# Soft-MoE experts stage: 256-column halves of the last weights, transposes moved, TensorE's order written out, filler products

## Chip, cores and metric

The kernel runs on one core of one Trainium2 chip, as one launch. The metric is the device time of one execution in microseconds; the median of three runs of the kernel before is 974.0 us (lowest 972.54, highest 979.01). Less is better.

## The reference

Three layers run one after the other; B is 8, H is 8, S is 576, N is 4608 tokens of 512 numbers.

```python
attn = softmax(mask(q @ k.T / 8)) @ v            # block-causal, blocks of 64
x = attn.transpose(0, 2, 1, 3).reshape(N, 512)
logits = x @ phi                                 # phi 512 x 32: 8 experts, 4 slots each
d = softmax(logits, axis=0)                      # over the tokens
slot_input = (d.T @ x).reshape(8, 4, 512)
for e in range(8):                               # w1[e] 512 x 1024, w2[e] 1024 x 512
    slot_out[e] = relu(slot_input[e] @ w1[e]) @ w2[e]
x = softmax(logits, axis=1) @ slot_out.reshape(32, 512)
h = relu(x @ w_in)                               # w_in 512 x 2048
out = (h * h) @ w_out                            # w_out 2048 x 512
```

The MoE weights are 32 MiB of float32 and `w_out` comes as 8 MiB of 64-bit floats (the device decodes them to float32), so the middle of the kernel moves much and computes little: 32 slots only.

## The kernel before, in words

**Stages.** `attention` (L195) runs over 32 pairs of heads (8 batches of 4). With each batch it updates a running maximum, a running sum `tot` and the running slot input `acc` (L69). `experts` (L1017) turns `acc` into slot outputs. `ffn` (L1196) is the long last stage: 96 steps of 18 products of 128x128 by 128x512 (L1306 to L1308), on TensorE alone nearly all of the time.

**The last batch's chain.** After the last pair the list `last` (L836 to L838) has one long chain of small steps: the logits of the last pair, `maxes` (VectorE), `running` (a transpose L726, then VectorE L728 to L731), `weights` (a product L737, VectorE, then ScalarE's exponentials L745 and L746), `total` (L786), `gather` (L815, L821), `invert` (L801, then VectorE L803 to L805), and the update of `acc` in four pieces (L828). `tokens` (L756) transposes the tokens of the batch beside it. Line 1013 issues what is left of the batch's work and then `last`, outside of the `manual_schedule` of L1009.

**Experts.** There are 32 weight chunks of 1 MiB (`wlist`, L147): 8 of `w1` for experts 0 to 3, 8 of `w1` for experts 4 to 7, 8 of `w2` for experts 0 to 3, and 8 of `w2` for experts 4 to 7. Each lies in a slot named by a letter (`slots`, L82). 19 chunks (RING) have a slot of their own; chunk 19 and on take a slot over when the products that read it are done. `after(r)` (L1079) issues the load of chunk r+19 behind the products of chunk r, on SyncE's queue, in the order of the chunks; behind chunk 31 come the first four tiles of `w_out` (`fetch_wo`, L1140), each MiB with 4 KB rows.

Chunks 0 to 23 are read from memory in rows of 2 KB. The last eight (L129 to L137) are quarters of columns: chunk c has column block `dt = c // 2` of 128 columns and one half of the 1024 rows of `w2`, for four experts; each of its four DMAs (256 KB, rows of 512 bytes) has 128 rows of all four experts. So each output block of 128 columns is complete after two chunks, is copied (L1130), transposed (`finish`, L1060) and folded with `w_in` into `psw` (`fold`, L1070: 4 products of 512 columns) while the next chunks come in. Behind the last chunk stand one copy, one transpose, one small copy (L1065) and one fold.

For each of four half layers the hidden values are copied with the Relu (L1096) and transposed at once (L1099). The softmax over experts for all tokens (`combine_a`, `combine_c` on VectorE, `combine_b` on TensorE: six transposes L1193 and a copy L1194 for each of six token groups) is spread over the chunks with `put`: `combine_b(g)` stands behind chunk 16+2g (CSTART 14, CSTEP 2).

**What sets TensorE's order.** Inside `manual_schedule` for TensorE (L1009) its instructions stay in the order of the program. Outside of it, in `experts` and `ffn` too, the compiler's scheduler orders them by its own estimate. The other engines' instructions are ordered by that scheduler in either case.

**Head of ffn.** L1208 issues the decoding of the first `w_out` tile (`decode_wo(0)`: one ScalarE and four VectorE steps, L154 to L180), then `psw` is split into `wf` (L1214 to L1219, ScalarE, VectorE and GpSimd), spread over the partitions (L1243), and the first hidden tile follows (L1252, L1262 to L1270).

A float32 product stands in the trace as two MATMUL records, one of a 16-bit type as one.

Of the kernel before, what the change touches and what calls it, by code (L numbers as in the profile page):

```python
# [23 lines left out]
def tile_attn_soft_moe_ffn(  # L24
# [27 lines left out]
    CSTART = 14  # L52
    CSTEP = 2
# [43 lines left out]
    nxt = [0]  # L97
    wots = {}
# [10 lines left out]
    def wchunk(i):  # L109
        kind, g, c = wlist[i]  # L110
        nm = slots[i]
        if nm in fixed:
            runs = [ar[:, 512 * q0:512 * (q0 + nq)] for ar, q0, nq in fixed[nm]]
        else:
            runs = [wpools[nm].tile([128, 2048], F32, tag="w", name="wch")]
        wt[i] = []
        fs = []
        for t in runs:
            nq = t.shape[1] // 512
            e0 = 4 * g + len(wt[i])  # L120
            es = slice(e0, e0 + nq)
            qs = [t[:, 512 * x:512 * x + 512] for x in range(nq)]
            wt[i] += qs
            if kind == 0:
                fh, dt = divmod(c, KD)
                src = w1[es, 128 * dt:128 * dt + 128, 512 * fh:512 * fh + 512].rearrange("e p f -> p e f")
            elif g == 0:
                src = w2[es, 128 * c:128 * c + 128, :].rearrange("e p f -> p e f")
            else:  # L129
                dt, kh = divmod(c, 2)  # L130
                for x in range(nq):
                    r0 = 512 * kh + 128 * (e0 - 4 * g + x)
                    src = w2[4 * g:4 * g + 4, r0:r0 + 128, 128 * dt:128 * dt + 128]
                    fs.append(lambda o=qs[x], src=src: nc.sync.dma_start(
                        out=o.rearrange("p (e f) -> p e f", e=4), in_=src.rearrange("e p f -> p e f")
                    ))
                continue  # L137
            if nm in "01" and i < RING:
                for x in range(nq):
                    fs.append(lambda o=qs[x], src=src[:, x]: nc.sync.dma_start(out=o, in_=src))  # L140
            else:
                fs.append(lambda t=t, src=src, nq=nq: nc.sync.dma_start(
                    out=t.rearrange("p (e f) -> p e f", e=nq), in_=src
                ))
        return fs
# [49 lines left out]
    def attention():  # L195
# [442 lines left out]
        def batch(b):  # L638
# [192 lines left out]

            if b == B - 1:
# [3 lines left out]
                    [lambda: logits_pair(3), maxes, running, groups] + [lambda u=u: tokens(u, 3) for u in range(5)]  # L836
                    + [recycle, weights, total] + [lambda u=u: gather(u) for u in range(4)] + [invert, lambda: gather(4)]
# [174 lines left out]
        nxt[0] += 1  # L1012
        for f in dq + work + half[1:] + last:
            f()
        st.close()

    def experts():  # L1017
# [19 lines left out]
        nc.vector.tensor_copy(si[:, :, 0:NSL], ps[:, 0:128].rearrange("p (a s) -> p a s", a=KD))  # L1037
        psw = ps_w.tile([128, 512], F32, tag="dx", name="psw")
# [4 lines left out]
        todo = {CSTART: [setup_sel]}  # L1043
# [4 lines left out]
        for g in range(NTILE // NG):  # L1048
            put(CA + g, lambda g=g: combine_a(g))
            put(CSTART + CSTEP * g, lambda g=g: combine_c(g))  # L1050
            put(
                CSTART + 2 + CSTEP * g,
                lambda g=g: combine_b(ps_e.tile([128, 1024], F32, tag="c", name="ps_c", bufs=1), g),
            )

# [28 lines left out]

        for g in range(2):
            for fh in range(2):
                for dt in range(KD):
                    for e4 in range(4):
# [4 lines left out]
                        )  # L1093
                    after(8 * g + KD * fh + dt)
                hs = ep.tile([128, 512], F32, tag="hs", name="hs")
                nc.scalar.activation(out=hs, in_=hp_[fh], func=AF.Relu)  # L1096
                pt = ps_e.tile([128, 512], F32, tag="a", name="ps_hT")
                for i in range(4):
                    nc.tensor.transpose(pt[:, 128 * i:128 * i + 128], hs[:, 128 * i:128 * i + 128], ident)  # L1099
                nc.vector.tensor_copy(  # L1100
                    hT[g][:, 4 * fh:4 * fh + 4], pt.rearrange("p (a e x) -> p a e x", a=4, e=4)[:, :, :, 0:SPE]
                )
        for kt in range(8):
            for e4 in range(4):
# [3 lines left out]
                )  # L1108
            after(16 + kt)
# [3 lines left out]
        for c in range(8):  # L1113
            dt, kh = divmod(c, 2)
            if kh == 0:
                po = ps_e.tile([128, 512], F32, tag=f"h{dt % 2}", name="po1", bufs=1)[:, 0:128]
                nc.vector.memset(po, 0.0)
            for k in range(4):
                for e4 in range(4):
                    nc.tensor.matmul(  # L1120
                        po[32 * e4:32 * e4 + SPE, :], hT[1][:, 4 * kh + k, e4, :], wt[24 + c][k][:, 128 * e4:128 * e4 + 128],
                        start=(kh == 0 and k == 0), stop=(kh == 1 and k == 3), tile_position=(0, 32 * e4),
                    )
# [3 lines left out]
            if kh == 0:  # L1127
                continue
            os_ = ep.tile([128, 128], F32, tag="os", name="os", bufs=2)
            nc.scalar.copy(os_, po)  # L1130
            pend.append(lambda dt=dt, os_=os_: (finish(1, [dt], os_), fold(dt)))
# [64 lines left out]
    def ffn():  # L1196
# [11 lines left out]
        for f in range(1):  # L1208
            for fn in decode_wo(f):
                fn()  # L1210
# [8 lines left out]
        nc.gpsimd.tensor_tensor(out=wf[1][:, p], in0=wfs, in1=wf[0][:, p], op=ALU.subtract)  # L1219
        psw_st.close()  # L1220
# [109 lines left out]
    with ExitStack():  # L1330
# [7 lines left out]
        experts()  # L1338
# [33 lines left out]
```

## Time and profile before

| what | value |
|---|---|
| median of 3 runs | 974.0 us (972.54 to 979.01) |
| the profiled execution's own time | 981.25 us |
| its span, first to last instruction | 979.5 us |
| TensorE busy in the span | 889.6 us (91%) |
| mean granted TensorE clock | 0.953 |

Times below are microseconds from the start of the profiled span. A row of the timeline has start, length, engine, line, operation, output<-inputs, shape and count, and in brackets the engine's idle time before it with what ended it. [...] The profiled execution took 7.25 us more than the median of the runs; 1.75 us of it lie around its span.

### The profile page before, as it was taken

Reading aid. Unit: us, or ns where it says so; the run is one execution under the profiler, and the core shown is the slowest. Engines: PE = TensorE matmul, PEld = TensorE weight load, DVE = VectorE, ACT = ScalarE, POOL = GpSimd, SP = SyncE. Lnnn points to the kernel's source line nnn. Section 1 sums busy time; section 2 is a strip of 40 time slices with the busy share of each in tenths; the row PEclk is TensorE's granted clock in tenths of the full one; section 3 lists DMA queues with packets and bytes.
Section 4 is the critical chain, followed back from the end, with each engine's and each line's share of the span. In section 5 each row is a group of like instructions: output and inputs, shape, how many; then the busy total and the mean of one; then the engine's idle time right before and its main releaser. Section 6 shows DMA issues by size and latency. Waiting matters only on the chain.

```text
span 979.5 us, 19573 instructions
## 1 busy us (share of the span) xinstructions
PE 889.6 (91%) x7712; PEld 658.3 (67%) x7712; DVE 595.2 (61%) x1359; ACT 514.6 (53%) x916; POOL 248.2 (25%) x390
## 2 busy tenths in 40 slices
PE   3758988999898998999897999999999999999997
PEld 2435656656575666667333777888888888888885
DVE  7746795878798796854631977544544444435342
ACT  5558775777676766644122957443434334334332
POOL 0313745436473646564000233000000000000000
PEclk9778998899899999999798999999999999999999
DMA  6768997797899766597899031100100101001002
GB/s 147 149 141 151 164 187 155 154 189 158 158 172 157 161 132 165 107 254 215 296 318 313 7 129 44 65 0 1 65 1 2 64 1 39 26 1 65 1 1 65
DMA packets 233629, 113.03 MB, mean 115 GB/s; under 512 B 194112, under 2 KB 210496, under 8 KB 233536
## 3 DMA queue, kind: packets, MB, share of 16 engines
q1 hardware_dynamic: 233536, 111.78, 49.4%
q8 instruction: 60, 0.98, 0.4%
q14 instruction: 33, 0.27, 0.1%
HBM read 78.71 MB, written 9.44 MB: 90 GB/s over the span
## 4 chain that ended last, share of the span: by engine, by line
PE 65%; DVE 9%; DMA 8%; ACT 6%; SPq 5%; POOL 4%; issue 2%; ACTq 0%; DVEq 0%
PE po L1306 12%; PE po L1308 12%; PE po L1307 12%; PE xm L558 5%; PE ps_sc L485 4%; PE ps_h L1252 3%; DMA raw<-in_moe_w_in_dram 2%; POOL ss L528 2%; PE ps_max L408 2%; PE ps_h L1090 2%; DVE pm L422 2%; PE ps_x L763 1%; POOL ul L668 1%; DMA s<-s 1%; SPq L287 1%
## 5 line engine op out<-in xcount | busy, mean ns | idle before, releaser
L1307 PE MATMUL po<-wol,gh 128*128 128x512 f32 x576 | 224.9, 391 | 2.0 <-POOL wol L1236 2.0
L1308 PE MATMUL po<-woh,gl 128*128 128x512 f32 x576 | 224.8, 391 | 0.0
L1306 PE MATMUL po<-woh,gh 128*128 128x512 f32 x576 | 224.0, 391 | 0.8 <-ACT woh L1235 0.7
L1262 ACT ACTIVATE r<-ps_h 128x768 f32<-128x768 f32 (+1 forms) x97 | 78.0, 806 | 204.4 <-PE ps_h L1252 204.4
L1269 DVE TENSOR_TENSOR sq<-r 128x768 f32<-128x768 f32 x80 | 76.7, 958 | 170.4 <-ACT r L1262 170.4
L523 ACT ACTIVATE p<-ps_sc,es 128x512 f32<-128x512 f32 x192 | 129.7, 695 | 52.4 <-PE ps_sc L494 33.6
L422 DVE TENSOR_REDUCE pm<-ps_max 128x4 f32<-128x512 f32 x160 | 107.6, 683 | 53.4 <-PE ps_max L416 52.8
L528 POOL TENSOR_TENSOR ss<-p 128x384 f32<-128x384 f32 (+1 forms) x128 | 84.6, 681 | 208.8 <-ACT p L523 208.6
L1306 PEld LDWEIGHTS po<-woh,gh 128*128 128x128 f32 x576 | 108.5, 189 | 24.5 <-ACT woh L1235 1.4
L1308 PEld LDWEIGHTS po<-woh,gl 128*128 128x128 f32 x576 | 108.4, 188 | 22.6
L1307 PEld LDWEIGHTS po<-wol,gh 128*128 128x128 f32 x576 | 108.6, 188 | 21.7 <-POOL wol L1236 2.6
L485 PE MATMUL ps_sc<-t,s 128*128 128x512 f16 (+3 forms) x512 | 110.9, 312 | 7.6 <-DMA s<-s 4.5
L528 POOL TENSOR_TENSOR ss<-ss,p 128x320 f32<-128x320 f32 (+1 forms) x128 | 98.4, 769 | 18.9 <-ACT p L523 7.6
L1270 DVE TENSOR_TENSOR gl<-sq,gh 128x768 fp32r<-128x768 f32 (+1 forms) x97 | 93.0, 959 | 16.3 <-ACT sq L1267 6.2
L558 PE MATMUL xm<-p,ar_hi 128*64 128x256 f32 (+3 forms) x512 | 94.3, 468 | 0.0
L1263 ACT ACTIVATE gh<-r 128x768 fp32r<-128x768 f32 (+1 forms) x97 | 81.6, 841 | 2.8
L408 PE MATMUL ps_max<-s,t 128*128 128x128 f16 (+3 forms) x256 | 63.7, 315 | 12.5 <-ACT t L396 6.8
L569 PEld LDWEIGHTS tl<-p,ar_hi 128*64 128x64 f32 x512 | 37.7, 143 | 39.0 <-issue 34.5
L494 PEld LDWEIGHTS <-s 128*128 128x128 f16 x512 | 46.8, 102 | 16.4 <-issue 4.0
L494 PE MATMUL ps_sc<-t,s 128*128 128x64 f16 x512 | 55.4, 197 | 1.0 <-ACT p L523 0.5
L1252 PE MATMUL ps_h<-cts,ws 128*128 128x512 f32 x192 | 50.3, 344 | 1.4 <-ACT r L1262 1.0
L485 PEld LDWEIGHTS <-s 128*128 128x128 f16 x512 | 37.9, 103 | 12.1 <-DMA s<-s 5.2
(210 smaller groups left out, 1356.0 us busy)
## 6 DMA issues: line engine op xcount, KB each, us to landing
wch<-in_moe_w_dram SPq DMA_DIRECT2D x12, 1024.0 KB, 8.5
ar_hi<-in_v_dram SPq DMA_DIRECT2D x64, 128.0 KB, 3.0
raw<-in_moe_w_in_dram SPq DMA_DIRECT2D x16, 512.0 KB, 5.3
wch<-in_moe_w_dram SPq DMA_DIRECT2D x32, 256.0 KB, 6.0
out_dram<-ot SPq DMA_DIRECT2D x32, 256.0 KB, 2.1
ar_hi<-in_moe_w_dram SPq DMA_DIRECT2D x6, 1024.0 KB, 7.6
s<-s SPq DMA_DIRECT2D x32, 144.0 KB, 3.3
ar_lo<-in_k_dram SPq DMA_DIRECT2D x32, 128.0 KB, 3.2
```

Source lines behind the costliest of these rows:

```text
L408: nc.tensor.matmul(ps[:, c0:c0 + 128 * (u + 1)].rearrange("p (s c) -> p s c", c=128), t1[:, 2 * u + hp, :], s1[:, hp:2 * u + 2:2, :], star ...
L422: nc.vector.tensor_reduce(out=o, in_=i, axis=AX.X, op=ALU.max)
L485: nc.tensor.matmul(ps[:, c0:c0 + w].rearrange("p (s c) -> p s c", c=128), kk[:, 2 * t + hp, :], qq[:, 2 * u0 + hp:8:2, :], start=(c0 == 0 ...
L494: nc.tensor.matmul(ps[:, c0:c0 + 64], kk[:, 2 * t + hp, :], qq[:, 8, h0:h0 + 64], start=(c0 == 0 and not second), stop=(second and last),)
L523: nc.scalar.activation(out=pt, in_=ps, func=AF.Exp, scale=es[:, 0:1])
L528: add = lambda o, x, y: nc.gpsimd.tensor_tensor(out=o, in0=x, in1=y, op=ALU.add)
L558: nc.tensor.matmul(box["xm"][64 * hp:64 * hp + 64, 128 * t:512], vs[:, t, hp, :], r, start=(t == 0), stop=(t == 3),)
L1263: nc.scalar.activation(out=gh[:, p], in_=r[:, p], func=AF.Square)
L1270: nc.vector.tensor_tensor(out=gl[:, p], in0=sq[:, p], in1=gh[:, p], op=ALU.subtract)
L1306: nc.tensor.matmul(pos[t], gh[:, sl], woh[f], start=(f == 0), stop=False)
L1307: nc.tensor.matmul(pos[t], gh[:, sl], wol[f], start=False, stop=False)
L1308: nc.tensor.matmul(pos[t], gl[:, sl], woh[f], start=False, stop=(f == KF - 1))
```

## The change

1. The last eight chunks become halves of 256 columns by quarters of the rows: rows of 1 KB, two DMAs of 512 KB for a chunk instead of four of 256 KB. A column half is complete after four chunks. Behind the last chunk stand a copy of 256 columns, two transposes and two folds. A chunk has 8 products of 256 columns instead of 16 of 128.
2. The transposes of the hidden values are held back (`late_t`) and issued behind the second chunk of the next half layer.
3. `combine_b(g)` moves from behind chunk 16+2g to behind chunk 24+g, `combine_c(g)` from chunk 14+2g to 23+g, `setup_sel` from 14 to 22.
4. `experts` and the leftover work behind the last pair run under `manual_schedule` for TensorE.
5. Fillers: `spin` issues products of 16-bit type with 256 columns on the identity's bits into a PSUM tile nobody reads: 10, 6, 6 and 4 in the last batch's chain, 4 more behind the slot input. In the chain the transposes of the last tokens now stand ahead of `maxes`.
6. In `ffn`, `decode_wo(0)` is issued behind the split of `psw` instead of ahead of it.

```diff
@@ tile_attn_soft_moe_ffn
-    CSTART = 14
-    CSTEP = 2
+    CSTART = 24
...
+    warm = ident.bitcast(F16)
+
+    def spin(ps, k):
+        for _ in range(k):
+            nc.tensor.matmul(ps[:, 0:256], warm[:, 0:128], warm, start=True, stop=True)
@@ wchunk
-                dt, kh = divmod(c, 2)
-                for x in range(nq):
-                    r0 = 512 * kh + 128 * (e0 - 4 * g + x)
-                    src = w2[4 * g:4 * g + 4, r0:r0 + 128, 128 * dt:128 * dt + 128]
-                    fs.append(lambda o=qs[x], src=src: nc.sync.dma_start(
-                        out=o.rearrange("p (e f) -> p e f", e=4), in_=src.rearrange("e p f -> p e f")
+                dh, kq = divmod(c, 4)
+                x = 0
+                while x < nq:
+                    y = e0 - 4 * g + x
+                    m = 1 if y % 2 or x + 1 == nq else 2
+                    r0 = 256 * kq + 128 * (y // 2)
+                    ea = 4 * g + 2 * (y % 2)
+                    src = w2[ea:ea + 2 * m, r0:r0 + 128, 256 * dh:256 * dh + 256]
+                    o = t[:, 512 * x:512 * (x + m)]
+                    fs.append(lambda o=o, src=src, m=m: nc.sync.dma_start(
+                        out=o.rearrange("p (e f) -> p e f", e=2 * m), in_=src.rearrange("e p f -> p e f")
                     ))
+                    x += m
@@ batch
+            def fill():
+                box["fill"] = ps_v.tile([128, 512], F32, tag="xm", name="ps_fill")
...
-                    [lambda: logits_pair(3), maxes, running, groups] + [lambda u=u: tokens(u, 3) for u in range(5)]
-                    + [recycle, weights, total] + [lambda u=u: gather(u) for u in range(4)] + [invert, lambda: gather(4)]
+                    [lambda: logits_pair(3), fill] + [lambda u=u: tokens(u, 3) for u in range(5)]
+                    + [maxes, lambda: spin(box["fill"], 10), running, groups, lambda: spin(box["fill"], 6)]
+                    + [recycle, weights, lambda: spin(box["fill"], 6), total]
+                    + [lambda u=u: gather(u) for u in range(4)] + [invert, lambda: gather(4), lambda: spin(box["fill"], 4)]
@@ attention
         with tc.manual_schedule(engines={mybir.EngineType.PE}):
             for n in range(N + 1):
                 pair(n)
-        nxt[0] += 1
-        for f in dq + work + half[1:] + last:
-            f()
+            nxt[0] += 1
+            for f in dq + work + half[1:] + last:
+                f()
@@ experts
+        spin(ps_e.tile([128, 512], F32, tag="a", name="ps_fill"), 4)
...
-        todo = {CSTART: [setup_sel]}
+        todo = {CSTART - 2: [setup_sel]}
...
-            put(CSTART + CSTEP * g, lambda g=g: combine_c(g))
             put(
-                CSTART + 2 + CSTEP * g,
+                CSTART + g,
                 lambda g=g: combine_b(ps_e.tile([128, 1024], F32, tag="c", name="ps_c", bufs=1), g),
             )
+        for g in range(NTILE // NG):
+            put(CSTART - 1 + g, lambda g=g: combine_c(g))
...
+        late_t = []
+
+        def turn_h(g, fh, hs):
+            pt = ps_e.tile([128, 512], F32, tag="a", name="ps_hT")
...
+                    if dt == 1 and late_t:
+                        late_t.pop()()
                     after(8 * g + KD * fh + dt)
                 hs = ep.tile([128, 512], F32, tag="hs", name="hs")
                 nc.scalar.activation(out=hs, in_=hp_[fh], func=AF.Relu)
-                pt = ps_e.tile([128, 512], F32, tag="a", name="ps_hT")
...
+                late_t.append(lambda g=g, fh=fh, hs=hs: turn_h(g, fh, hs))
         for kt in range(8):
...
+            if kt == 1:
+                late_t.pop()()
...
         for c in range(8):
-            dt, kh = divmod(c, 2)
-            if kh == 0:
-                po = ps_e.tile([128, 512], F32, tag=f"h{dt % 2}", name="po1", bufs=1)[:, 0:128]
+            dh, kq = divmod(c, 4)
+            if kq == 0:
+                po = ps_e.tile([128, 512], F32, tag=f"h{dh}", name="po1", bufs=1)[:, 0:256]
                 nc.vector.memset(po, 0.0)
-            for k in range(4):
+            for y in range(2):
                 for e4 in range(4):
+                    c0 = 256 * (e4 % 2)
                     nc.tensor.matmul(
-                        po[32 * e4:32 * e4 + SPE, :], hT[1][:, 4 * kh + k, e4, :], wt[24 + c][k][:, 128 * e4:128 * e4 + 128],
-                        start=(kh == 0 and k == 0), stop=(kh == 1 and k == 3), tile_position=(0, 32 * e4),
+                        po[32 * e4:32 * e4 + SPE, :], hT[1][:, 2 * kq + y, e4, :],
+                        wt[24 + c][2 * y + e4 // 2][:, c0:c0 + 256],
+                        start=(kq == 0 and y == 0), stop=(kq == 3 and y == 1), tile_position=(0, 32 * e4),
                     )
...
-            if kh == 0:
+            if kq < 3:
                 continue
-            os_ = ep.tile([128, 128], F32, tag="os", name="os", bufs=2)
+            os_ = ep.tile([128, 256], F32, tag="os", name="os", bufs=1)
             nc.scalar.copy(os_, po)
-            pend.append(lambda dt=dt, os_=os_: (finish(1, [dt], os_), fold(dt)))
+            dts = [2 * dh, 2 * dh + 1]
+            pend.append(lambda dts=dts, os_=os_: [finish(1, dts, os_)] + [fold(dt) for dt in dts])
@@ ffn
-        for f in range(1):
-            for fn in decode_wo(f):
-                fn()
...
         nc.gpsimd.tensor_tensor(out=wf[1][:, p], in0=wfs, in1=wf[0][:, p], op=ALU.subtract)
+        for fn in decode_wo(0):
+            fn()
@@ the caller
-        experts()
+        with tc.manual_schedule(engines={mybir.EngineType.PE}):
+            experts()
```

## Rows read from the trace of the kernel before

**Rows 1.** Page, second part: granted TensorE clock in tenths, 40 slices of 24.5 us.

```profile
PEclk9778998899899999999798999999999999999999
```

**Rows 2.** Windows (start:end, us, busy us (count) of five engines, PEclk, DMA share, GB/s).

```profile
472.00:485.00 13.00, 11.02 (x66) 4.56 (x69) 7.67 (x34) 1.14 (x4) 0.30 (x1) 0.50 0.69 243
...
530.00:540.00 10.00, 8.15 (x37) 3.93 (x30) 4.22 (x8) 4.97 (x13) 2.17 (x2) 0.51 0.92 369
...
480.00:484.00 4.00, 4.00 (x24) 0.96 (x20) 3.92 (x20) 0.63 (x2) 0.00 (x0) 0.50 0.52 186
484.00:497.00 13.00, 11.48 (x93) 3.45 (x86) 6.29 (x32) 2.98 (x7) 0.00 (x0) 0.96 1.01 370
...
498.00:531.00 33.00, 28.70 (x417) 13.11 (x409) 5.33 (x24) 6.77 (x11) 0.00 (x0) 0.98 1.06 277
...
526.00:530.00 4.00, 1.46 (x32) 0.44 (x32) 0.00 (x0) 0.00 (x0) 0.00 (x0) 0.94 0.95 269
```

**Rows 3.** Timeline of TensorE, the last batch's chain.

```profile
470.52 0.33 PE L726 MATMUL ps_mx<-ident,mx 128*128 128x128 f32 x1 [0.88 <-DVE mx L721]
471.62 0.63 PE L737 MATMUL ps_nb<-ident,nm 32*128 32x32 f32 x2 [0.77 <-DVE nm L731]
473.06 0.47 PE L786 MATMUL ps_ds<-ones,d 128*32 128x1 f32 x10 [0.81 <-ACT d L746]
...
475.85 0.65 PE L821 MATMUL ps_dx<-xe,d 64*32 64x128 f32 x8
477.22 1.89 PE L1034 MATMUL ps_si<-em,acc 128*128 128x32 f32 x8 [0.71 <-DVE em L805]
479.56 1.94 PE L1090 MATMUL ps_h<-ar_hi,si 128*32 128x512 f32 x8 [0.45 <-DVE si L1037]
```

**Rows 4.** The chain of waits, 430 to 580 us (start, us, what).

```profile
473.54 1.87 PE ps_dx L815 x8
...
479.56 7.24 PE ps_h L1090 x34
...
487.39 3.60 PE ps_h L1090 x31
```

**Rows 5.** Timeline of TensorE, 443 to 456 us, at the full clock.

```profile
447.24 1.06 PE L815 MATMUL ps_dx<-x,d 128*32 128x512 f32 x8
...
455.71 0.38 PE L485 MATMUL ps_sc<-t,s 128*128 128x256 f16 x2
455.93 0.22 PE L494 MATMUL ps_sc<-t,s 128*128 128x64 f16 x2
```

**Rows 6.** Timeline of SyncE's queue (merged issues of loads).

```profile
481.55 4.83 SPq L142 DMA_DIRECT2D ar_hi<-in_moe_w_dram  x4
490.15 0.37 SPq L142 DMA_DIRECT2D wch<-in_moe_w_dram  x1
491.01 34.34 SPq L134 DMA_DIRECT2D wch<-in_moe_w_dram  x32
```

**Rows 7.** DMA view, 498 to 524 us, 512-byte rows (packets, MB, share).

```profile
q1 hardware_dynamic: 14222, 7.07, 107.3%
```

**Rows 8.** DMA view, 485 to 497 us, memory rows of 2 KB.

```profile
q1 hardware_dynamic: 2294, 4.44, 100.6%
```

**Rows 9.** Timeline of TensorE, end of the experts stage and head of ffn.

```profile
530.66 0.61 PE L1120 MATMUL po<-wch,hT 128*4 128x128 f32 x8 [0.22 <-DMA wch<-in_moe_w_dram]
531.65 0.47 PE L1064 MATMUL ps_soT<-ident,os 128*128 128x128 f32 x1 [0.39 <-ACT os L1130]
532.39 1.93 PE L1072 MATMUL psw<-tin,so 128*32 128x512 f32 x8 [0.27 <-DVE so L1065]
...
537.86 2.46 PE L1243 MATMUL ps_ws<-wf,sel 128*128 128x384 f32 x6 [0.24 <-POOL wf L1219]
540.16 0.63 PE L1306 MATMUL po<-woh,gh 128*128 128x512 f32 x2
```

**Rows 10.** Timeline of TensorE, 500 to 580 us, one group of moved transposes.

```profile
503.25 0.71 PE L1193 MATMUL ps_c<-ident_r,cs 128*128 128x128 f32 x6
```

More of the change, by code (lines that the diff above doesn't have):

```diff
@@ L1083, in after @@
                 fetch_wo(r - 19)
+        late_t = []
+        def turn_h(g, fh, hs):
+            pt = ps_e.tile([128, 512], F32, tag="a", name="ps_hT")
+            for i in range(4):
+                nc.tensor.transpose(pt[:, 128 * i:128 * i + 128], hs[:, 128 * i:128 * i + 128], ident)
+            nc.vector.tensor_copy(
+                hT[g][:, 4 * fh:4 * fh + 4], pt.rearrange("p (a e x) -> p a e x", a=4, e=4)[:, :, :, 0:SPE]
+            )
         for g in range(2):
@@ L1096, in experts @@
                 nc.scalar.activation(out=hs, in_=hp_[fh], func=AF.Relu)
-                pt = ps_e.tile([128, 512], F32, tag="a", name="ps_hT")
[L1098 to L1102, printed above, removed]
+                late_t.append(lambda g=g, fh=fh, hs=hs: turn_h(g, fh, hs))
         for kt in range(8):
```

## The prediction

> **What bounds the kernel now.** I read the page's slices first: the granted clock is below full in several slices up to the middle of the span and at nine tenths or more in the last half, where `ffn` keeps TensorE busy [rows 1]. The change touches only the stretch between the last batch's chain and the head of `ffn`, so I cut this stretch with windows. [...] And the DMA engines are full (share 1.01 to 1.06) from 484 to 531 us, but move 370 GB/s while the 2 KB rows run and 277 GB/s while the 512-byte rows run; from 480 to 484 us they are half empty [rows 2]. Then I read who ends last. SyncE issues chunks 19 to 22 from 481.55 to 486.38 us, chunk 23 at 490.15 and the 32 small DMAs from 491.01 to 525.35 us [rows 6]; TensorE waits for the last of these until 530.66 us, and from there a chain of small steps leads to the first product of `ffn` at 540.16 us [rows 9]. So the end of this stage is set by the transfer of the weights, and its start by TensorE's chain, which releases the slots.
>
> **Part 1, the last batch's chain and the clock.** TensorE stands idle ahead of four steps of the chain for 0.88, 0.77, 0.81 and 0.71 us and ahead of the first chunk for 0.45 us, together 3.6 us; the clock is at the low level through what follows [rows 2, 3]. A filler product of 256 columns takes about 0.11 us at the full clock: two of that form start 0.22 us ahead of the next instruction [rows 5]. So 30 of them are 3.3 us and lie in these 3.6 us; the first ten (1.1 us against 0.88 us of idle) may push the chain by 0.2 us, and at the low clock all 30 would be 6.6 us. I take it that the clock stays up. Then the eight `gather` products cost 1.06 us as in an earlier batch and not 1.87 [rows 4, 5]: 0.8 us. The eight products of L1034 (1.89 us) and the short ones of L737 and L821 (0.63, 0.65) would be about half, but VectorE's pieces of `acc` pace L1034: I take 1.6 us for all, bounds 0.5 and 2.0. So the first chunk starts some 2.4 us earlier, at 477.2. The first 34 records of L1090 take 7.24 us and 31 later ones 3.60 [rows 4], 0.116 each: 3.9 us at the full clock, 3.3 us less.
>
> What that is worth is read at the DMA queue. Chunk 19's issue waits for chunk 0's products; these end at 477.2 + 0.9 = 478.1 instead of 481.55, and chunks 20 to 22 follow in 0.93 us each, faster than they are transferred. So the engines are full from about 479.7 instead of 484: the stream of the remaining 13 chunks starts 4.3 us earlier. If the clock falls for chunks 0 to 3 alone, this shrinks by 0.7 us only, since 1.7 us a chunk is still under the 2.8 us that a MiB takes at 370 GB/s.
>
> **Part 2, rows of 1 KB.** The view of the DMA packets gives a price for each size: 26 us x 16 engines x 1.073 / 14222 = 31.4 ns for rows of 512 bytes, and 12 x 16 x 1.006 / 2294 = 84 ns for rows that are nearly all of 2 KB [rows 7, 8]. No row shows 1 KB. On the straight line between the two it is 31.4 + 52.6 / 3 = 49 ns. The bounds are 63 ns (no gain per byte) and 42 ns (the 2 KB price per byte). The eight chunks are 8.39 MB; at the 277 GB/s of now they take 30.3 us [rows 2]. At 49 ns for 1 KB instead of 63 this is 30.3 x 49 / 63 = 23.6 us, 6.7 us less (0 to 10 by the bounds). I take the line, since a fixed part in each packet explains both rows. There are 16 issues instead of 32; SyncE's queue was behind the engines, not ahead of them, so this saves nothing by itself.
>
> [...]
>
> So the last weights land 4.3 + 6.7 = 11.0 us earlier, at about 519.7.
>
> **Part 3, is TensorE then late?** Its work from 477.2: 24 chunks of 0.93 (22.3), four times four transposes (2.6, hidden behind other products now, so the copies' waits of some 0.8 us each go), eight chunks of two 0.46 halves (7.4), six groups of `combine_b` at 0.71 [rows 10] (4.3), and transposes and two folds of the first half (2.8): 516.6 without any wait. That is 3 us ahead of the transfer, so the moved `combine_b` groups cost nothing: they stand in waits for weights. The cover is thin: if the transfer gains 3 us more, TensorE's own work sets the end. In the order of the program the folds stand behind chunk 28, which waits for its weights, and nothing but chunks 29 to 31 waits for them.
>
> **Part 4, the tail and the head.** From 530.66 to the fold's end (532.39 + 1.93) it was 3.7 us, at the low clock [rows 2, 9]. Now two transposes and two folds stand there: at the full clock about 3.8 us, at the low one 5.7. In the last two chunks TensorE has 0.9 us of work in each 3 us, about as thin as from 526 to 530, where the clock fell [rows 2]. I take the middle, 1.0 us lost. From the fold's end to the first product of `ffn` it is 5.8 us, of which TensorE's 2.46 and others run at half speed [rows 9]. At the full clock 1.3 us may go; `decode_wo(0)` behind the split may put up to 0.7 us of ScalarE into it. I take 0.5 gained. The rest, 439 us, is `ffn` at full clock and does not change; its `w_out` tiles are queued behind chunk 31 as before and move with it.
>
> **The sum.** 4.3 + 6.7 - 1.0 + 0.5 = 10.5 us of the span of 979.5, so 969.0, and 970.7 with the 1.75 us around it. The median of the runs is 7.25 us under the profiled execution; taken from it, 974.0 - 10.5 = 963.5. A change of 1% is 9.7 us, about what a measurement of this kernel can tell from no change.
>
> **Rivals.**
> - Longer rows bring nothing per byte. For it: the engines are full in both stretches [rows 2], and a limit behind them would not show. Against it: the price per packet above. Then 4.3 - 1.0 + 0.5 = 3.8 remain: 970.2.
> - The transfer is cheaper than the line, 42 ns: 4.3 + 10.0 would land the last weights at 516.4, where TensorE's own work ends as well: 14.3 less 1.8 for waits on each other, tail and head is 12.5: 961.5.
> - The fillers do not hold the clock. For it: it fell where TensorE was idle between short steps, not wholly idle. Then the fillers at the low level are 6.6 us against 3.6 of idle; with most behind waits some 1 us is lost, the early start goes, and 6.7 - 1.0 - 1.0 + 0.5 = 5.2 remain: 968.8.
> - Slower: TensorE's fixed order lets it wait at each chunk of the last eight with its other work queued behind, and the clock falls at the first of these waits and stays low. From chunk 24 (502 us) TensorE has about 7.4 + 4.3 + 2.8 + 3.8 = 18.3 us of work; at 1.85 times that (7.24 / 34 against 3.60 / 31) it is 33.9 us and the last fold ends at 535.9 instead of 534.3. It decides if the low level holds from chunk 24 on; from chunk 16 on it is 7.9 x 0.85 = 6.7 us more. The middle of the two, with `decode_wo` behind it: 980. For it: the clock fell in waits of just this kind at 529 [rows 2]. Against it: the moved transposes fill these waits, and between 485 and 529 us the clock was full. [...]
>
> **How the numbers follow.** The forecast has 0.55 with a range of its own of 961.5 to 966.5 (tail and head by their bounds, 1 KB between 45 and 53 ns); no gain from the rows 0.10, the cheap rows 0.15, the lost clock 0.15, slower 0.05. The range takes the first, the cheap rows and the lost clock: 959.5 to 969.5. Under 964.3 lie two thirds of the forecast and all of the cheap rows: 0.52. Within 1% are the rest of the forecast, no gain and the lost clock, 0.43. Slower 0.05.
>
> **What would show it right or wrong.** Right: a granted clock of 1.00 from 471 to 485 us; the first chunk near 477 us; SyncE's issue of the four reused slots from about 478; a rate near 350 GB/s while the 1 KB rows run; the last wait for weights near 520; the first product of `ffn` near 530. The forecast is wrong if the rate stays under 300 GB/s, if the clock falls in the chain in spite of the fillers, or if TensorE's last products wait for ScalarE or VectorE and not for DMA.

## The result, and the profile after

The changed kernel takes 966.2 us (median of 6 runs, 959.8 to 967.9) beside 975.2 us for the kernel before on the same chip (6 runs, 972.4 to 979.0): a ratio of 0.990 (95% interval 0.986 to 0.994). The forecast was 10.5 us less; the medians are 9.0 us apart. The profiled execution took 967.0 us with a span of 965.2 us, 14.3 us less than the span before.

Of these 14.3 us not all belong to the change. The row transpose of the running maximum, which opens the chain of the last batch, starts at 470.52 us in [rows 3] and at 465.97 us in the first fence below: 4.55 us earlier, from an attention part that the change leaves alone. In the profiled executions of all the kernels here this instruction starts anywhere between 461.3 and 470.5 us (470.5 is the kernel before). So everything below is counted from the start of this instruction ("from the maximum").

The timeline of TensorE in the kernel after; columns as in [rows 3], which it answers, and then [rows 9]:

```profile
465.97 0.29 PE L737 MATMUL ps_mx<-ident,mx 128*128 128x128 f32 x1
466.09 0.82 PE L101 MATMUL ps_fill<-ident 128*128 128x256 f16 x6
467.02 0.40 PE L748 MATMUL ps_nb<-ident,nm 32*128 32x32 f32 x2
467.36 0.83 PE L101 MATMUL ps_fill<-ident 128*128 128x256 f16 x6
468.24 0.39 PE L797 MATMUL ps_ds<-ones,d 128*32 128x1 f32 x10
...
471.00 1.09 PE L1050 MATMUL ps_si<-em,acc 128*128 128x32 f32 x8 [0.17 <-DVE em L816]
471.92 0.60 PE L101 MATMUL ps_fill<-ident 128*128 128x256 f16 x4
472.59 3.64 PE L1119 MATMUL ps_h<-ar_hi,si 128*32 128x512 f32 x32
...
507.73 1.92 PE L1091 MATMUL psw<-tin,so 128*32 128x512 f32 x16 [0.28 <-DVE so L1084]
...
513.95 0.61 PE L1149 MATMUL po<-wch,hT 128*4 128x256 f32 x8 [0.89 <-DMA wch<-in_moe_w_dram]
515.43 0.84 PE L1149 MATMUL po<-wch,hT 128*4 128x256 f32 x8 [0.86 <-DMA wch<-in_moe_w_dram]
516.79 0.69 PE L1083 MATMUL ps_soT<-ident,os 128*128 128x128 f32 x2 [0.52 <-ACT os L1160]
517.77 3.64 PE L1091 MATMUL psw<-tin,so 128*32 128x512 f32 x16 [0.28 <-DVE so L1084]
...
526.49 0.39 PE L1336 MATMUL po<-woh,gh 128*128 128x512 f32 x1
```

The waits of 0.7 to 0.9 us of [rows 3] are gone: the fillers of L101 stand where they were. The first chunk's products start 6.62 us from the maximum instead of 9.04, and 32 of them take 3.64 us, 0.114 each, where 34 took 7.24. At the other end the wait for the last weights ends at 515.43, 49.46 us from the maximum instead of 60.14, and the first product of `ffn` starts at 60.52 instead of 69.64: 9.1 us earlier. From there to the end of the span it is 438.7 us; before it was 439.3.

Windows of the kernel after (columns as in [rows 2]):

```profile
472.00:485.00 13.00, 12.93 (x117) 4.25 (x119) 10.94 (x53) 3.27 (x9) 0.00 (x0) 1.00 0.98 362
485.00:498.00 13.00, 13.00 (x126) 4.37 (x118) 1.22 (x5) 1.46 (x3) 0.00 (x0) 1.00 1.07 360
498.00:512.00 14.00, 11.33 (x135) 4.91 (x137) 4.05 (x17) 4.43 (x7) 0.00 (x0) 1.00 1.09 348
512.00:524.00 12.00, 8.70 (x55) 2.75 (x48) 3.44 (x7) 3.31 (x7) 1.28 (x2) 0.65 0.99 384
524.00:530.00 6.00, 6.00 (x24) 4.91 (x24) 4.35 (x8) 5.95 (x13) 0.23 (x1) 0.84 0.03 12
```

The granted clock is 1.00 in the windows up to 512 us, where before it was 0.50 from 472 to 485. DMA is at a share of 0.98 or more from 472 to 524 us; before it was 0.69 from 472 to 485. In the last window but one the clock is 0.65: it fell at 515.7 us, just as the last weights came, and so the last two folds of L1091 take 3.64 us and not 1.92 as the first two at 507.73.

The page's slices of the granted clock answer to [rows 1]; low tenths are now left in the attention part and in one slice, from 507 to 531 us:

```profile
PEclk9778999999899999999997999999999999999999
```

SyncE's queue in the kernel after, in answer to [rows 6]:

```profile
473.72 2.94 SPq L153 DMA_DIRECT2D ar_hi<-in_moe_w_dram  x4
479.59 0.37 SPq L153 DMA_DIRECT2D wch<-in_moe_w_dram  x1
480.45 27.68 SPq L144 DMA_DIRECT2D wch<-in_moe_w_dram  x16
```

Chunk 19 is issued 7.75 us from the maximum instead of 11.03, and 16 DMAs stand for the last eight chunks instead of 32. The DMA view of the kernel after, 492 to 512 us, in answer to [rows 7]:

```profile
q1 hardware_dynamic: 6976, 6.93, 108.5%
```

The price of a packet that is nearly always 1 KB is 20 us x 16 engines x 1.085 / 6976 = 49.8 ns.

### The profile page after: what moved, and what is told of

It reads as the page before. It is cut to its first block, busy times and chain, and to the rows that moved or that the text cites. A ratio compares the mean times of both kernels' runs of the same rounds, so it can differ in the third digit from the quotient of the medians.

```text
span 965.2 us, 19357 instructions
## 1 busy us (share of the span) xinstructions
PE 878.1 (91%) x7614; PEld 650.1 (67%) x7614; DVE 596.4 (62%) x1355; ACT 514.5 (53%) x914; POOL 249.0 (26%) x390
## 3 DMA queue, kind: packets, MB, share of 16 engines
q1 hardware_dynamic: 225088, 111.77, 49.8%
## 4 chain that ended last, share of the span: by engine, by line
PE 64%; DVE 11%; DMA 9%; ACT 5%; POOL 4%; SPq 3%; issue 3%; DVEq 0%; ACTq 0%
PE po L1336 12%; PE po L1338 12%; PE po L1337 12%; PE xm L569 5%; PE ps_sc L496 4%; PE ps_h L1282 3%; DMA raw<-in_moe_w_in_dram 3%; DVE pm L433 2%; POOL ss L539 2%; PE ps_max L419 2%; PE ps_h L1119 1%; POOL ul L679 1%; PE tl L580 1%; PE ps_x L774 1%; DMA s<-s 1%
```

## The experiments

The theory behind the forecast: two parts of the change earn the time, the rows of 1 KB (the stream is shorter) and the fillers (the clock stays up, so the stream starts earlier); TensorE's order, the moved transposes and `combine` groups and the place of `decode_wo` earn nothing. The rivals are told in the expectations. The views give the granted clock as a share of the full one, and no run shows a frequency: where two expectations below say 1.2 and 2.4 GHz, the runs show 0.50 and 1.00. The table has the profiled execution of each kernel, in us from the maximum: start of the first chunk's products, landing of the last weights, end of the last fold, first product of `ffn`; then the time from the landing of chunk 23 to the last one's ("stream"), and where TensorE's clock was low between the maximum and 545 us (us of the execution, with the length). The ratio is to the kernel before on the same chip as the run.

| kernel | first chunk | last landing | last fold | `ffn` | stream | low clock | ratio to before (95%) |
|---|---|---|---|---|---|---|---|
| before | 9.04 | 60.09 | 63.81 | 69.64 | 31.8 | 471.5 (13.7), 529.5 (10.2) | 1 |
| after | 6.63 | 49.42 | 55.44 | 60.53 | 24.8 | 515.7 (10.2) | 0.990 (0.986 to 0.994) |
| after, run again | 6.63 | 49.20 | 54.26 | 58.56 | 24.0 | 518.8 (3.4) | 0.991 (0.988 to 0.994) |
| 1 KB rows alone | 9.04 | 52.40 | 56.73 | 61.16 | 24.2 | 467.0 (13.7) | 0.993 (0.990 to 0.996) |
| after, no fillers | 8.80 | 53.10 | 56.95 | 61.37 | 24.0 | 465.9 (10.2), 506.9 (6.8) | 0.995 (0.993 to 0.997) |
| after, 512-byte rows | 6.63 | 55.93 | 58.42 | 64.57 | 31.0 | 506.0 (10.2), 523.0 (6.8) | 0.996 (0.993 to 0.998) |
| order alone | 8.81 | 58.67 | 62.12 | 68.28 | 30.7 | 466.2 (10.2), 510.6 (6.8), 524.2 (10.2) | 1.000 (0.997 to 1.002) |
| rows and fillers alone | 6.64 | 48.96 | 52.80 | 58.40 | 23.9 | 517.1 (3.4) | 0.985 (0.982 to 0.988) |

**1 KB rows alone.** The kernel before with the halves of 256 columns (two DMAs a chunk, two folds at a time) and nothing else.

```diff
+                    src = w2[ea:ea + 2 * m, r0:r0 + 128, 256 * dh:256 * dh + 256]
...
-            if kh == 0:
+            if kq < 3:
                 continue
```

> The kernel before with the 1 KB rows alone (two DMAs of 512 KB a chunk, two folds behind the last chunk); no fillers, TensorE's order and the combine groups as before. Theory A (the stream of the last weights and its start set the end): the 16 DMAs take about 1.55 us each, 24.8 us instead of 31.8, 7.0 less; the tail at the low clock has a second fold, 2.3 more; so 4.5 us faster than before, ratio 0.995. Rival B (TensorE's order gives the gain, the transfer is hidden anyway): no gain, ratio 1.00 to 1.003.

966.8 us, and the stream takes 24.2 us instead of 31.8. The first chunk starts where it did before. So the rows alone take 7.6 us from the stream, without any filler.

**No fillers.** The changed kernel without its 30 products.

```diff
     def spin(ps, k):
-        for _ in range(k):
-            nc.tensor.matmul(ps[:, 0:256], warm[:, 0:128], warm, start=True, stop=True)
+        pass
...
```

> The changed kernel without any of the 30 fillers. Theory A: the clock falls in the last batch's chain as before, the first chunk starts 2.4 us later and chunks 0 to 3 run at 1.2 GHz, the four reused slots are issued 3.2 us later and the last weights land 3 to 3.6 us later; 3 us slower than the changed kernel, ratio to before about 0.993. Rival C (fillers cost what they give; the fixed order alone holds the clock): no difference from the changed kernel, ratio 0.990.

967.4 us. Its timeline of TensorE has the waits of [rows 3] back, and the low clock with them:

```profile
464.24 0.33 PE L736 MATMUL ps_mx<-ident,mx 128*128 128x128 f32 x1 [0.88 <-DVE mx L731]
465.34 0.40 PE L747 MATMUL ps_nb<-ident,nm 32*128 32x32 f32 x2 [0.77 <-DVE nm L741]
466.56 0.48 PE L796 MATMUL ps_ds<-ones,d 128*32 128x1 f32 x10 [0.81 <-ACT d L756]
...
470.71 1.88 PE L1049 MATMUL ps_si<-em,acc 128*128 128x32 f32 x8 [0.71 <-DVE em L815]
473.04 5.15 PE L1117 MATMUL ps_h<-ar_hi,si 128*32 128x512 f32 x32 [0.45 <-DVE si L1052]
```

The first chunk starts 2.2 us later than with fillers and the last weights land 3.7 us later. So what holds the clock in the chain is the fillers, not the order: in the ten profiled executions of kernels that have them (each kernel once, the changed one twice) it is full there (1.00 from 472 to 485 us in the kernel after), in the four without them it falls (0.50 in the kernel before).

**512-byte rows.** The changed kernel with the old quarters of 128 columns.

```diff
-                    src = w2[ea:ea + 2 * m, r0:r0 + 128, 256 * dh:256 * dh + 256]
...
+                    src = w2[4 * g:4 * g + 4, r0:r0 + 128, 128 * dt:128 * dt + 128]
...
```

> The changed kernel with the last eight chunks in quarters of 128 columns again (512-byte rows, 32 DMAs, one fold behind the last chunk), all else as changed. Theory A: the stream takes 7.0 us more, the tail at the low clock 2.3 less; 4.7 us slower than the changed kernel, ratio to before about 0.995. Rival B (order): within 1 us of the changed kernel, 0.990.

968.1 us. The early start stays, the stream is 31.0 us again, and the last weights land 6.5 us later than in the kernel after. Its `ffn` starts only 4.0 us later than there, because the tail is 3.5 us shorter (2.49 us from the landing to the last fold's end instead of 6.02): one fold at the full clock stands behind the last chunk, not two at the low one.

**Order alone.** The changed kernel without fillers and with 512-byte rows: what stays is TensorE's fixed order, the moved transposes and `combine` groups, and `decode_wo(0)` behind the split.

```diff
-        for _ in range(k):
-            nc.tensor.matmul(ps[:, 0:256], warm[:, 0:128], warm, start=True, stop=True)
+        pass
...
-                    src = w2[ea:ea + 2 * m, r0:r0 + 128, 256 * dh:256 * dh + 256]
...
+                    src = w2[4 * g:4 * g + 4, r0:r0 + 128, 128 * dt:128 * dt + 128]
...
```

> The changed kernel without fillers and with 512-byte rows: what is left is TensorE's order, the moved transposes, the moved combine groups and decode_wo's place. Theory A: the stream sets the end as before; first product 69 to 70 us behind the maximum's transpose, ratio to before 0.999 to 1.001. Rival B: 2 us or more faster.

972.7 us beside 972.6: no difference. `ffn` starts 1.4 us earlier in the profiled execution, with three stretches of low clock.

**Rows and fillers alone.** The kernel before with the 1 KB rows, the 30 fillers and the leftover work of the chain under TensorE's fixed order; the transposes, the `combine` groups, the experts' order and `decode_wo` as before.

```diff
+            nxt[0] += 1
+            for f in dq + work + half[1:] + last:
+                f()
...
+        spin(ps_e.tile([128, 512], F32, tag="a", name="ps_fill"), 4)
```

> The kernel before with the 1 KB rows and the 30 fillers alone (and the last batch's steps in program order, which the fillers need); the transposes, the combine groups, the scheduler's order in the experts stage and decode_wo as before. Theory A: the same as the changed kernel, first product of ffn 59.5 to 61 us behind the maximum's transpose, ratio 0.990. Rival B (the fixed order and the moved transposes carry part of the gain): over 62 us, ratio 0.994 or more.

960.4 us, 0.985 (0.982 to 0.988): all of the gain is there without the moved parts. It is even more than expected: 0.990 lies outside this interval, and `ffn` starts at 58.40 us and not at 59.5 or later. Only one wait for weights is left on TensorE near the end, and the folds run at the full clock, as its timeline shows:

```profile
506.90 2.56 PE L1139 MATMUL po<-wch,hT 128*4 128x256 f32 x41
510.28 0.62 PE L1139 MATMUL po<-wch,hT 128*4 128x256 f32 x8 [0.83 <-DMA wch<-in_moe_w_dram]
511.44 0.44 PE L1082 MATMUL ps_soT<-ident,os 128*128 128x128 f32 x2 [0.54 <-ACT os L1150]
512.15 1.92 PE L1090 MATMUL psw<-tin,so 128*32 128x512 f32 x16 [0.28 <-DVE so L1083]
```

The next runs ask whether the clock in the last chunks, where the forecast was 1.3 us off, can be held, and what that is worth.

**Fillers ahead of the last halves.** The changed kernel with eight fillers ahead of each half of chunk 31 and some behind.

```diff
+                if c == 7:
+                    spin(ft, 8)
...
+        spin(ft, 5)
```

> The changed kernel with more fillers at the end of the experts stage: 8 ahead of each half of the last chunk, 5 behind it, 3 between the last transposes and the folds. Theory A: the clock stays at 2.4 GHz through the last folds and the head of ffn; the tail takes 4.1 us instead of 6.0, the head 4.3 instead of 5.1; 2.0 to 2.7 us faster than the changed kernel, ratio to before about 0.9875. Rival D (the tail and head are paced by ScalarE, VectorE and GpSimd and not by TensorE's clock): under 0.5 us.

963.4 us, 0.990 (0.987 to 0.994); the last fold ends 5.42 us behind the landing, not the 4.1 expected. A miss with two causes, both in its timeline:

```profile
507.83 3.60 PE L1091 MATMUL psw<-tin,so 128*32 128x512 f32 x16 [0.28 <-DVE so L1084]
...
514.60 1.05 PE L101 MATMUL ps_fill<-ident 128*128 128x256 f16 x8
515.57 0.62 PE L1151 MATMUL po<-wch,hT 128*4 128x256 f32 x8
516.12 1.05 PE L101 MATMUL ps_fill<-ident 128*128 128x256 f16 x8
517.10 0.61 PE L1151 MATMUL po<-wch,hT 128*4 128x256 f32 x8
```

Here the clock fell earlier, at 507.8, in the waits of chunks 27 and 28, and the first two folds took 3.60 us. TensorE then came late to chunk 31, whose weights had landed at 515.5, and the fillers stood in the way of its products.

**Fillers in all the waits.** Six (or two) fillers ahead of the halves of chunks 27, 28 and 31.

```diff
+                if c in (3, 4, 7):
+                    spin(ft, 6 if y or c == 7 else 2)
```

> The changed kernel with fillers in the waits for weights: 2 ahead of the first and 6 ahead of the second half of chunks 27 and 28, 6 ahead of each half of chunk 31, 4 behind it, 2 between the last transposes and the folds. In the run with fillers at the end alone the clock fell at the waits of chunks 27 and 28, the first two folds took 3.60 us and TensorE came late to chunk 31. Theory A: with these waits filled the clock stays up from the chain to the end; both pairs of folds take 1.9 us, the last weights' landing to the last fold's end 3.9 to 4.2 us, from there to the first product of ffn 4.4 us; first product 58.0 us behind the maximum's transpose instead of 60.5; ratio to before about 0.987. Rival D (tail and head paced by other engines, fillers in the way): not under 59.5 us, ratio 0.990 or more.

962.9 us, 0.988 (0.985 to 0.991). The clock holds through the last fold, which ends 3.84 us behind the landing, 2.2 less than in the kernel after; then it falls in the head of `ffn`, which takes 5.5 us and not the 4.4 expected, and so `ffn` starts at 58.83 us instead of 58.0.

**Rows of 2 KB.** One DMA of 1 MiB for each of the last eight chunks, all 512 columns at once; the four folds come behind chunk 31.

```diff
+                src = w2[es, 128 * c:128 * c + 128, :].rearrange("e p f -> p e f")
...
+        pend.append(lambda: [finish(1, range(KD), os_)] + [fold(dt) for dt in range(KD)])
```

> The changed kernel with the last eight chunks as whole rows of 2 KB like the eight before them (one DMA of 1 MiB a chunk, one output block of 512 columns, four transposes and four folds behind the last chunk), all else as changed. Theory A: the price per packet goes on falling, the stream takes 22.0 us instead of 24.8; behind the last weights stand 0.9 of products, 0.6 copy, 0.7 transposes and 3.7 of folds, 6.5 us at the full clock and up to 12 at the low one instead of 6.0; so 0 to 3 us slower than the changed kernel, ratio 0.990 to 0.993. Rival E (only the stream's length matters): 2.8 us faster, 0.987.

964.2 us, 0.991 (0.987 to 0.994), as the changed kernel. Its window from 480 to 498 us, columns as in [rows 2]:

```profile
480.00:498.00 18.00, 18.00 (x164) 6.22 (x164) 3.31 (x15) 2.74 (x5) 0.00 (x0) 1.00 1.05 386
```

It moves 386 GB/s, and the last weights land 46.47 us from the maximum, 3.0 earlier than in the kernel after; but four transposes and four folds stand behind them, as the timeline of TensorE shows:

```profile
510.45 1.04 PE L1130 MATMUL po<-wch,hT 128*4 128x512 f32 x8 [1.66 <-DMA wch<-in_moe_w_dram]
512.25 1.07 PE L1068 MATMUL ps_soT<-ident,os 128*128 128x128 f32 x4 [0.75 <-ACT os L1138]
513.63 4.67 PE L1076 MATMUL psw<-tin,so 128*32 128x512 f32 x32 [0.32 <-DVE so L1069]
```

From the landing to the last fold's end it is 7.9 us, with the clock low for 3.4 of them, and `ffn` starts at 59.24: 1.3 us earlier than in the kernel after, 0.7 later than when that was run again. What the longer rows save, the longer tail takes for the greater part or wholly.

**`combine` groups back, without and with fillers.** Is it the new place of these groups that leaves TensorE empty at the end? The changed kernel with the old start and step, and the same with 12 fillers around the last half.

```diff
-    CSTART = 24
+    CSTART = 14
+    CSTEP = 2
...
+                if c == 7 and y:
+                    spin(ft, 6)
```

> The changed kernel with the combine groups back behind chunks 16 to 26 (CSTART 14, CSTEP 2), all else as changed. Theory F (moved behind the last chunks the groups are no cover: TensorE gets through chunk 24 some 4 us earlier and then waits for the weights with thin work, and the clock falls): at the old places TensorE meets the weights only at the last chunk or two, the clock stays up to the last landing, both pairs of folds take 1.9 us, landing to the last fold's end 3.8 us; first product of ffn 58 to 58.8 us behind the maximum's transpose; ratio to before 0.985 to 0.987. Theory A as forecast (the groups lie in waits and cost nothing): 60 to 61 us, 0.990.

> The run with the combine groups back, with fillers at the end of the experts stage besides: 6 ahead of the second half of the last chunk, 4 behind it, 2 between the last transposes and the folds. Theory F: the clock has not fallen there anyway; the head of ffn keeps the clock more often; 0 to 0.8 us faster than without, ratio 0.985. If fillers stand in the way: landing to the last fold's end over 4.2 us.

Without fillers 965.1 us, 0.990 (0.987 to 0.993), with them 961.5 us, 0.986 (0.983 to 0.989). Theory F was missed in the first: the groups' place alone does not settle the clock. The timeline without fillers shows a wait at each half of the last chunks, and the low clock from the last one on:

```profile
514.18 0.61 PE L1148 MATMUL po<-wch,hT 128*4 128x256 f32 x8 [0.42 <-DMA wch<-in_moe_w_dram]
515.69 0.62 PE L1148 MATMUL po<-wch,hT 128*4 128x256 f32 x8 [0.89 <-DMA wch<-in_moe_w_dram]
517.19 0.61 PE L1148 MATMUL po<-wch,hT 128*4 128x256 f32 x8 [0.89 <-DMA wch<-in_moe_w_dram]
518.68 1.03 PE L1148 MATMUL po<-wch,hT 128*4 128x256 f32 x8 [0.87 <-DMA wch<-in_moe_w_dram]
520.26 0.69 PE L1082 MATMUL ps_soT<-ident,os 128*128 128x128 f32 x2 [0.54 <-ACT os L1159]
521.23 3.64 PE L1090 MATMUL psw<-tin,so 128*32 128x512 f32 x16 [0.28 <-DVE so L1083]
```

With the fillers the same place reads:

```profile
512.34 0.62 PE L1150 MATMUL po<-wch,hT 128*4 128x256 f32 x8 [0.89 <-DMA wch<-in_moe_w_dram]
512.89 0.83 PE L102 MATMUL ps_fill<-ident 128*128 128x256 f16 x6
513.83 0.62 PE L1150 MATMUL po<-wch,hT 128*4 128x256 f32 x8
...
515.71 1.92 PE L1090 MATMUL psw<-tin,so 128*32 128x512 f32 x16
```

Six of them (0.83 us) fill the wait without moving the products behind it, and the two folds take 1.92 us instead of 3.64. In the two other kernels with six fillers in this wait ("fillers in all the waits" and the next one) the clock held through the last fold as well (two folds in 1.92 us in both).

**Fillers in the head of `ffn` too.** The last kernel with 11 more fillers between the first products of `ffn`, under TensorE's fixed order.

```diff
+            spin(ft, 3)
             spread(0, parts[0])
+            spin(ft, 3)
             hid[0] = hidden(*seq[0], mid=lambda: store_wo(0))
+            spin(ft, 5)
```

> As the run before, with TensorE's order written out in the head of ffn too and 3, 3 and 5 fillers there, in its waits of 0.38, 0.35 and 0.41 us. Theory G (the head's clock fall of 0.7 to 1.7 us comes from these short waits): no fall between the last landing and the steady part of ffn, last fold's end to the first product 4.4 us; ratio 0.983 to 0.985. Rival D (head paced by ScalarE, VectorE and GpSimd): 4.4 us or more with the fillers in the way, no gain over the run before.

Beside it the changed kernel ran once more, with no edit:

> The changed kernel as it is, beside these runs on the same chip, so that they are compared with it and not only with the kernel before. All theories: ratio to before 0.990; landing to the last fold's end 3.8 to 6.0 us with where the clock falls.

966.0 us, 0.991 (0.988 to 0.993) with the 11 fillers, beside 966.6 us for the changed kernel run again. The first one's profiled execution has no low clock at all behind the maximum and the earliest `ffn` of all, 57.62 us from the maximum. Yet it was not measured faster than the run without the 11 fillers (961.5 us), and its expectation of 0.983 to 0.985 was missed. One row says why a part of it may be lost: the products soon wait for a decoded tile (timeline of TensorE).

```profile
532.50 1.19 PE L1345 MATMUL po<-woh,gh 128*128 128x512 f32 x4 [0.90 <-ACT woh L1269]
```

The kernel after has a wait of 0.98 us at the same tile. In the profiled executions, whose spans differ by 3.9 us (965.4 and 961.5), the difference lies ahead of the maximum: it starts at 468.98 us here and at 464.79 us without the 11 fillers, in an attention part that the edit leaves alone. From the maximum to the end of the span the kernel with them is 0.3 us shorter. Whether the 4.5 us between the two medians lie there too cannot be told from one execution of each, and stays open.

## Why the prediction was right, and where a size was off

- **The chain and the clock** (part 1). The clock held, as forecast. The first chunk starts 2.4 us earlier (forecast 2.4), its products take half the time (34 records at 0.114 us are 3.4 us less; forecast 3.3), and chunk 19 is issued 3.3 us earlier (forecast 3.45). The run without fillers shows that they are the cause of the full clock and of most of the earlier start: of the 2.4 us, 0.2 are there without them (8.80 instead of 9.04).
- **The start of the stream.** Forecast 4.3 us earlier. Chunk 23 lands 3.7 us earlier in the kernel after, 3.1 when it was run again. The step from the issue of chunk 19 (3.3 us) to 4.3 was too generous: in the kernel after chunks 19 to 23 land 3.1 to 3.7 us earlier, about as much as chunk 19 is issued earlier, and there was not a further microsecond to win.
- **The rows** (part 2). Forecast 6.7 us from 49 ns a packet; the view gives 49.8 ns, and the stream took 7.0 us less in the kernel after and 7.6 to 7.9 in the other runs with such rows. With that the last landing is 10.7 us earlier (run again 10.9; forecast 11.0): the two terms were off by 0.3 to 1.2 us each, in opposite directions; that their sum came within 0.3 us is in part luck. At a full share of the DMA engines the views have 277 GB/s with rows of 512 B (the kernel before), 348 with 1 KB (the kernel after) and 386 with 2 KB ("rows of 2 KB").
- **TensorE is not late** (part 3). It waits for weights at chunks 27, 28 and 31, at each half of the last one by 0.9 us, so its own work was ahead as worked out. That the moved groups cost nothing is shown only for 512-byte rows, and there only together with the other moved parts: "order alone", 1.000 (0.997 to 1.002). With rows of 1 KB, where there is less cover (a stream of 24 us instead of 31), the groups at their old places took 965.1 us beside 966.6 on the same chip, which is no clear difference; and "rows and fillers alone" (0.985) leaves room for a cost of all the moved parts together.
- **The tail** (part 4) is the term that was mis-sized. Forecast: 1.0 us lost, the middle between folds at the full and at the low clock. Measured: 6.02 us instead of 3.71 from the landing to the last fold's end, 2.3 lost, with the folds wholly at the low clock. Run again it was 5.06, since there the clock fell during the folds. So the clock fell ahead of the folds in one execution and within them in the other, and the loss of 1.0 was too small by 0.4 to 1.3 us. Both kernels in which the scheduler orders the experts stage ("1 KB rows alone" and "rows and fillers alone") held the clock through the last folds without fillers there (1.92 us in both); of the kernels with the fixed order, 1 KB rows and no fillers at the end, three executions of four lost it there (after, run again, groups back; in "no fillers" it had fallen earlier, at 506.9 us). So the fixed order, with its wait at each half, is a suspect for this loss; no run tests it alone. The head gave 0.8 us in the kernel after (5.08 instead of 5.84) and 1.5 run again; forecast 0.5. At the full clock it takes 4.4 us with `decode_wo(0)` ahead of the split ("1 KB rows alone", 4.43) as with it behind ("no fillers", 4.42): the 0.7 us that the forecast allowed for this move are not there. Tail and head together: 1.5 lost, or 0.2 gained, where the forecast had 0.5 lost.
- **The sum.** 10.67 - 2.31 + 0.76 = 9.1 us in the profiled execution, 10.89 - 1.35 + 1.54 = 11.1 us in the second one; the forecast of 10.5 lies between, and the medians differ by 9.0.
- **The rivals.** That longer rows bring nothing fell with "512-byte rows" (the stream goes back to 31.0 us). A price of 42 ns would have made a stream of 31.8 x 42 / 63 = 21 us; none with rows of 1 KB was under 23.9. The fillers held the clock in the chain. The slower case needs a clock that falls at the first waits and stays low: it did fall in such waits, as early as 506.0 us in "512-byte rows" and 506.9 in "no fillers", but for 3.4 to 10.2 us each time and partly with weights still to come behind it; it cost the tail 1.2 to 2.4 us where two folds of 1 KB rows stand there and nothing is in their way (5.06 to 6.23 us instead of 3.84), and every kernel with the longer rows was measured under the time before (0.985 to 0.995, no interval reaching 1).
- **What the change leaves.** "Rows and fillers alone" (960.4 us) and "`combine` groups back, with fillers" (961.5 us) have lower medians than both kernels of this case. The second was run beside the changed kernel (966.6 us), and their intervals overlap at one edge (0.983 to 0.989 against 0.988 to 0.994). The first ran on another chip than the changed kernel run again. The profiled executions place these differences for the most part outside of the stretch that was changed. "Rows and fillers alone" has a span 6.1 us shorter than the kernel after: 4.7 us of it lie ahead of the maximum, 2.1 between the maximum and the first product of `ffn` (the tail at the full clock). "`combine` groups back, with fillers" has one 4.6 us shorter than the changed kernel run again: 2.3 us lie ahead of the maximum, 0.1 in the stretch, 2.2 behind it, where the changed kernel's clock was low for 3.4 us from 566.6 us. So it is not shown that the moved parts or the fillers at the end make the 5 us.

## What to carry to other kernels

Find what the end of a stage waits for, and price a transfer by its packets: a straight line through two packet sizes of the same trace gave the third to one or two nanoseconds (49 against 49.8 by the view and 46.9 by the stream). In these runs fillers were free inside a wait that was there in any case (six, 0.83 us, in one of 0.9 us); ahead of products whose data had come already they stood in the way (eight, 1.05 us, in "fillers ahead of the last halves"), and behind short waits that they left open the clock fell in some executions, just ahead of the work that counted (at 507.8 us in the same run, ahead of two folds that took 3.60 us). Compare kernels from a mark behind the part that the change leaves alone: here that part alone varied by 9 us. Longer rows also mean coarser pieces, so count what stands behind the last one before taking the longest (7.9 us with rows of 2 KB, 2.49 with 512 B).

## What the runs showed of the hardware that was not expected

- Where the clock falls is not fixed by the program. The same kernel fell at 515.7 us for 10.2 us in one execution and at 518.8 us for 3.4 us in another, so the time from the last landing to the last fold was 6.02 or 5.06 us; at the full clock it was 3.84 in five other kernels and 4.33 in "1 KB rows alone", where TensorE was still busy with earlier chunks when the last weights came. A term that depends on it is a range.
- Short waits can be enough for it to fall: in the fence of the `combine` groups without fillers the eight products at 518.68 us took 1.03 us instead of 0.61, behind waits of 0.42, 0.89, 0.89 and 0.87 us with 0.6 us of products between them. They do not always lower it: in the kernel after the waits at chunks 27 and 28 were as long (up to 0.90), and the folds behind them still took 1.92 us. Products of 256 columns whose result nobody reads, put into the last such wait, held it in both kernels that have the groups back and these fillers: the last two folds took 1.92 us, and the window from 512 to 524 us of "fillers in the head of `ffn` too" is at 1.00.
- A packet of 1 KB took 49.8 ns by the view of the kernel after and 24.0 us x 16 / 8192 = 46.9 ns by the stream when it was run again; the straight line had 49.
